# Splitting a table's product between VectorE and GpSimd, loading two factors a table sooner, and moving filling products into the prologue

## The chip, the cores and the metric

The kernel runs on one core of a Trainium2 chip. The metric is the device time of one execution in microseconds; lower is better. TensorE multiplies matrices, VectorE and ScalarE work on tiles, GpSimd does small tiles and indirect transfers, and SyncE's queue (SP) issues most of the loads.

## The reference, cut to what matters

Three stages follow one another: a recurrent attention, a mixture of eight experts, and a dense two-layer network.

```
for t in range(S):                      # S = 768, 4 x 8 heads, 40 x 40 states
    y[t]  = r[t] @ state
    Sa    = state @ a[t]
    state = state * w[t] - outer(Sa, b[t]) + outer(v[t], k[t])
x = attention rows, 3072 x 320
x = gate * eom * (relu(x @ w1[e]) @ w2[e])      # e = argmax(x @ w_gate)
out = g(x @ w_in) @ w_out                       # 320 -> 2048 -> 320
```

The change touches the attention alone.

## The kernel before, in words

The sequence is cut into 12 chunks of 64 steps, and the heads into two halves, so there are 24 steps `s` with 16 heads each (8 in each half of the partitions). What a step needs apart from the state is made ahead of time, in what is called a table here. Table `s` is made by `stepA1(s)` and `stepA1b(s)`, all on VectorE:

- a scan over the factors `w`, backwards, gives `F`, the products of the factors up to the chunk's end (L608, 128x520);
- the reciprocal of eight of its columns goes into `d1` (L612), and the same columns are kept as `e64` (L613);
- a second scan, over the factors and `d1`, gives `e` (L616);
- `kf` is `k` and `b`, each multiplied by `F` (L621, 128x1024, of the form 8 x 2 x 64);
- `g` is `a` multiplied by `e` (L627, 128x512).

TensorE then forms the table's 64x64 products `L` from `kf` and `g` (`a2L`, L637) and transposes `kf` (`a2kbp`, L653). ScalarE copies from them, and VectorE multiplies one of them with a mask (`a2ka`, L646, one input in PSUM). Every fourth table a 32x32 triangular inverse is worked out on VectorE. It is a list of small multiplications (L692) and subtractions (L694) between SBUF tiles. `tick()`, called after most other VectorE instructions, takes one of them from the list, and `due()` runs those that must be done by a given step. The result is transposed (L706) for the products `W` of `slot`.

Eight tables (0 to 7) are made in the prologue. Then `slot(s)` runs for each step. It does the step's own products and those of the step before it, and near its end makes table `s+9`; slot 0 makes table 8 as well. The order on each engine is the order in which the program calls; nothing reorders it. The 17th and later slots make no tables. After the attention come the experts and the dense network, in which TensorE is busy nearly without a break.

The inputs of a table lie in one buffer, `fms[0]`, in three pieces: the factors (columns 0 to 520), `k` and `b` (521 to 1544), and `a` (1545 to 2056). `loadAn()` issues the six transfers of the next table on SP's queue behind the table in work. Each waits there until the instruction that reads the piece is done, and each later one waits behind it. `rzs[1]`, `xt` and others are buffers that the slots use later; ScalarE clears them in the prologue.

`heat(n)` issues `n` products of the identity with itself on TensorE, whose result nobody reads. There are 12 at the start, 8 in slot 0 ahead of the first products `W`, and 4 further on in slot 0.

GpSimd has few instructions in the attention: it clears the lower triangle of the inverse, and from the tenth slot on issues the indirect transfers that scatter rows to the experts.

Of the kernel before, what the change touches and what calls it, by code (L numbers as in the profile page):

```python
# [11 lines left out]
F32 = mybir.dt.float32  # L12
# [8 lines left out]
MUL, ADD, SUB = ALU.mult, ALU.add, ALU.subtract  # L21
P = 128
# [524 lines left out]
def attention(ctx,octx,tc,a,m,ident,rp):  # L547

    nc=tc.nc
    FM,R,VM,VX,VT=a["FM"],a["R"],a["VM"],a["VX"],a["VT"]  # L550
# [6 lines left out]
    ep=early.enter_context(tc.tile_pool(name="early",bufs=1,side="right"))  # L557
# [2 lines left out]
    psL=first.enter_context(tc.tile_pool(name="psL0",bufs=2,space=PSUM))  # L560

    LA=8
    NFM=1; NG=LA+1; NX=2; NR=2
    def persist(n,shape,nm,cp=cp):
        r=[]
        for i in range(n):
            t=cp.tile(shape,F32,name=f"{nm}{i}")
            r.append(t)
        return r
    fms=persist(NFM,[P,521+1024+512],"fm",ep)  # L570
    ones1=ep.tile([P,8,65],F32,name="ones1"); d1=ep.tile([P,8,65],F32,name="d1")
    mask=cp.tile([P,64],F32,name="mask")

    gs=persist(NG-3,[P,8,64],"g")+persist(3,[P,8,64],"gx",ep)
    kas=persist(3,[P,8,64],"kx",ep)+persist(LA-3,[P,8,64],"ka")
    xs=persist(NX,[P,2,4,232],"x")
    rzs=persist(NR,[P,2,4,2,64],"rz")
    mcs=persist(2,[P,8,64],"mc")
    xt=cp.tile([P,4,256],F32,name="xt")
    la=deque(range(NST))  # L580
    def loadAn():
        if la: loadA(la.popleft())
    FMP=(slice(0,521),slice(521,1545),slice(1545,2057))
    def loadA(s):
        c,up=divmod(s,2); f=fms[s%NFM]

        for cs in FMP:
            for sd in range(2): nc.sync.dma_start(out=f[64*sd:64*sd+40,cs],in_=FM[c,up,sd,:,cs])
    for cs in FMP: nc.sync.dma_start(out=fms[0][:,cs],in_=a["F0"][0,:,cs])
    la.popleft()  # L590
    nc.vector.memset(ones1,0.0); nc.vector.memset(ones1[:,:,64:65],1.0)
    nc.gpsimd.memset(d1,0.0)
# [2 lines left out]
    def clear(t):  # L595
        t=t.rearrange("p "+" ".join("abcd"[:len(t.shape)-1])+" -> p ("+" ".join("abcd"[:len(t.shape)-1])+")")
        n=t.shape[1]; m=next(m for m in range(D,0,-1) if n%m==0)
        nc.scalar.copy(t.rearrange("p (a b) -> p a b",b=m),z[:,0:m].unsqueeze(1).to_broadcast([P,n//m,m]))
# [3 lines left out]
    E={};KBt={};NT={};N01={};TT={};E64={};yts={};MT={}  # L602

    KF={}; fence=[None]
    def stepA1(s):
        f=fms[s%NFM]
        F=ep.tile([P,521],F32,tag="F1" if s in (1,3) else "F",name="F",bufs=1)
        nc.vector.tensor_tensor_scan(F[:,519::-1],f[:,520:0:-1],ones1.rearrange("p q t -> p (q t)")[:,::-1],0.0,MUL,ADD)  # L608
        F3=F[:,0:520].rearrange("p (q t) -> p q t",q=8)
        tick()  # L610
        e64=ring.tile([P,8,1],F32,tag="e64",name="e64",bufs=LA+3)
        nc.vector.reciprocal(d1[:,:,0:1],F3[:,:,0:1])  # L612
        nc.vector.tensor_copy(e64,F3[:,:,0:1])  # L613
        tick()
        e=ring.tile([P,8,65],F32,tag="e",name="e",bufs=LA+2)
        nc.vector.tensor_tensor_scan(e.rearrange("p q t -> p (q t)"),f[:,0:520],d1.rearrange("p q t -> p (q t)"),0.0,MUL,ADD)  # L616

        tick()
        if s in (1,3,5): kf=xt.rearrange("p a (b h t) -> p (a b) h t",b=2,h=2)
        else: kf=ep.tile([P,8,2,64],F32,tag="kf",name="kf",bufs=1)  # L620
        nc.vector.tensor_tensor(kf,f[:,521:1545].rearrange("p (q h t) -> p q h t",q=8,h=2),F3[:,:,1:65].unsqueeze(2).to_broadcast([P,8,2,64]),MUL)  # L621
        KF[s]=kf;E[s]=e;E64[s]=e64
        tick()
    def stepA1b(s):
        f=fms[s%NFM]; g=gs[s%NG]; e=E[s]
        A3=f[:,1545:2057].rearrange("p (q t) -> p q t",q=8)
        nc.vector.tensor_tensor(g,A3,e[:,:,0:64],MUL)  # L627
        tick()
    LP={}
    def a2L(s):  # L630
        g=gs[s%NG]; kf=KF[s]
        L=LP[s]=[psL.tile([P,8,64],F32,tag=f"L{i}",name=f"L{i}") for i in range(2)]
        for q in range(8):
            for i in range(2):
                for sd in range(2):
                    h=sd^i; sl=slice(64*sd,64*sd+64)
                    nc.tensor.matmul(L[i][64*h:64*h+64,q],kf[sl,q,h],g[sl,q],start=(q==0),stop=True,skip_group_check=True)  # L637
        if s%4==0: NT[s//4]=ep.tile([P,4,8,32],F32,tag="nt",name="nt",bufs=1)
        N01[s]=ring.tile([P,8,32],F32,tag="n01",name="n01",bufs=LA+1)
    def a2ev(s,sd):  # L640
        L=LP[s][0]; nt=NT[s//4][:,s%4]; n01=N01[s]; b0=64*sd
        nc.scalar.mul(nt[b0:b0+32],L[b0:b0+32,:,0:32],-1.0)
        nc.scalar.mul(nt[b0+32:b0+64],L[b0+32:b0+64,:,32:64],-1.0)
        nc.scalar.copy(n01[b0:b0+32],L[b0:b0+32,:,32:64])
    def a2ka(s):
        nc.vector.tensor_tensor(kas[s%LA],LP[s][1],mask.unsqueeze(1).to_broadcast([P,8,64]),MUL)  # L646
        tick()
    def a2kbp(s):
        kf=KF[s]; r=[]
        for h in range(2):  # L650
            kbp=ps.tile([P,4,128],F32,tag="ps",name="kbp"); r.append(kbp)
            for q in range(4):
                nc.tensor.transpose(kbp[:,q],kf[:,4*h+q].rearrange("p h t -> p (h t)"),ident)  # L653
        return r
    def a2kb(s,r):
        kb=KBt[s]=ring.tile([P,8,128],F32,tag="kb",name="kb",bufs=LA+1)
        for h in range(2): fence[0]=nc.scalar.copy(kb[:,4*h:4*h+4],r[h])
    m.tick=lambda: tick()
    invq=deque(); fine=[]; end=[]; WARM=12
    def tick():  # L660
        if left[0] or rest()<=lim[0]: return
        if not fine and invq: fine.extend(invq.popleft())
        if fine: fine.pop(0)(False)
    def inv(n):
        while fine: fine.pop(0)(False)
        for _ in range(min(n,len(invq))):
            for f in invq.popleft(): f(True)
        if not invq and end: end.pop()()
    lim=[0]
    def rest(): return len(fine)+2*len(invq)  # L670
# [60 lines left out]
    def loadX(s):  # L731
        c,up=divmod(s,2)
        for sd in range(2):
            vl=slice(64-64*sd,128-64*sd)
            nc.sync.dma_start(out=xs[s%NX][vl,sd].rearrange("p a d -> p (a d)"),in_=VX[c,up,sd])

    def loadVT(s):
        c,up=divmod(s,2)
        for j in range(2):
            nc.sync.dma_start(out=xt[64*j:64*j+40,:,64:192],in_=VT[c,up,j].rearrange("d (a t) -> d a t",a=4))  # L740
    def loadR(s):
        c,up=divmod(s,2)
        rz=rzs[s%NR]
        for j in range(2):
            nc.sync.dma_start(out=rz[64*j:64*j+40,j].rearrange("p a b c -> p (a b c)"),in_=R[c,up,j])
# [15 lines left out]
    def slot(s):  # L761
        B=s<NST; Y=s>0; n2=s+LA if s+LA<NST else None
        if B:
            c,up=divmod(s,2)
# [4 lines left out]
            for q in range(8):  # L769
                for sd in range(2):  # L770
                    sl=slice(64*sd,64*sd+64)
                    i=nc.tensor.matmul(R1[sl,q],g[sl,q],mc[sl,q,0:40],start=False,stop=False,skip_group_check=True)
# [14 lines left out]
        if s==0:  # L787
            a2L(LA-1)
            a2ev(LA-1,0)
            stepA1(LA); stepA1b(LA); loadAn(); a2ka(LA-1)  # L790
            heat(8)
        if Y:
            s1=s-1
            c1,up1=divmod(s1,2)
# [88 lines left out]
        if s+LA+1<NST: stepA1(s+LA+1); stepA1b(s+LA+1)  # L883
# [35 lines left out]
    def heat(n):  # L919
        warm=ps.tile([P,512],F32,tag="ps",name="warm")  # L920
        for _ in range(n): nc.tensor.matmul(warm[:,0:128],ident,ident,start=True,stop=True)
    heat(WARM)
    stepA1(0); stepA1b(0); loadAn()
    kbp={}
    for s in range(4):
# [13 lines left out]
    for s in range(4,LA):  # L939
        if s<LA-1:  # L940
            a2L(s)
            for sd in range(2): a2ev(s,sd)
        if s<LA-1: a2kb(s,a2kbp(s))
        if s<LA-1: stepA1(s+1); stepA1b(s+1); loadAn(); a2ka(s)
        inv(4)
    clear(xt); loadVT(0); loadX(1); loadR(1)
    clears=m.clear(z)
    inv(100)
# [5 lines left out]
    for s in range(NST+1):  # L954
        slot(s)
        if s==NST-5: early.close(); m.open(octx)
        if s>NST-5: m.early()
        if s==NST-1: m.first()
# [4 lines left out]
def body(tc,a):  # L963
    nc=tc.nc
    with ExitStack() as ctx, tc.manual_schedule():
        cp=ctx.enter_context(tc.tile_pool(name="cp",bufs=1))
        ident=cp.tile([P,P],F32,name="ident")
        m=Moe(ctx,tc,a,ident,cp)
        rp=ctx.enter_context(tc.tile_pool(name="rp",bufs=1))
        with ExitStack() as actx: rq=attention(actx,ctx,tc,a,m,ident,rp)  # L970
        m.open2(ctx)
        m.go(rq)
# [25 lines left out]
```

## Time and profile before

| | us |
|---|---|
| median of three runs (983.27 to 986.19) | 984.25 |
| the profiled execution | 983.8 |
| its span, first to last instruction | 982.1 |
| TensorE busy | 929.9 |
| VectorE busy | 758.5 |
| GpSimd busy | 154.7 |

Busy times are sums over the whole span. What an engine does in one stage has to be read from the rows of that stage. An engine's instructions start a little before the one in front has ended, so the time that an instruction adds is read from start to start.

### The profile page before, as it was taken

How to read it: one execution, taken by the hardware profiler on the slowest of the kernel's cores; microseconds unless marked ns; L12 is line 12 of the kernel's file. 1: busy time of each engine (PE TensorE's matmuls, PEld its weight loads, DVE VectorE, ACT ScalarE, POOL GpSimd, SP SyncE). 2: the span in 40 equal slices, each digit the busy share in tenths (PEclk: the TensorE clock that was granted, in tenths of full speed). 3: DMA queues.
4: the chain of work that ended last, by engine and by line, in shares of the span. 5: the costliest groups of instructions: out<-in, count | busy, mean ns of one | idle time of the engine just before them, and what ended most of it. 6: DMA issues, size and time to landing. Idle time of an engine off the chain costs nothing. (4 is left out here: it accounts for less than half of the span.)

```text
span 982.1 us, 26651 instructions
## 1 busy us (share of the span) xinstructions
PE 929.9 (95%) x11140; PEld 849.1 (86%) x11140; DVE 758.5 (77%) x1715; ACT 400.1 (41%) x823; POOL 154.7 (16%) x246
## 2 busy tenths in 40 slices
PE   6469999999999999999999999899999999999998
PEld 5458888888889999899999998779999999999997
DVE  7999899999998556688888886677766666666655
ACT  3736445555553443655556554332212221212211
POOL 1000000111011114144434443101010010100000
PEclk7569899999999999999999999899999999999999
DMA  4434677445433643677777766311000010000000
GB/s 125 123 107 152 214 215 233 129 134 144 123 95 95 189 134 108 224 235 231 233 239 230 247 224 193 123 47 28 28 22 33 1 30 25 27 27 1 28 1 27
DMA packets 59390, 118.45 MB, mean 121 GB/s; under 512 B 7492, under 2 KB 34308, under 8 KB 59268
## 3 DMA queue, kind: packets, MB, share of 16 engines
q1 hardware_dynamic: 55220, 103.04, 34.7%
q0 software_dynamic: 4048, 13.69, 4.1%
q8 instruction: 88, 1.44, 0.6%
q14 instruction: 34, 0.28, 0.1%
HBM read 90.24 MB, written 26.46 MB: 119 GB/s over the span
## 5 line engine op out<-in xcount | busy, mean ns | idle before, releaser
L394 PE MATMUL hp<-xh,w 128*128 128x512 f32 (+3 forms) x1008 | 298.9, 379 | 0.5 <-DVEq L248 0.3
L421 PE MATMUL yp<-w,hh 128*128 128x320 f32 (+1 forms) x1280 | 284.3, 309 | 0.6 <-ACT hh L410 0.6
L421 PEld LDWEIGHTS yp<-w,hh 128*128 128x128 f32 (+1 forms) x1280 | 217.0, 185 | 11.5 <-ACT hh L410 2.2
L394 PEld LDWEIGHTS hp<-xh,w 128*128 128x128 f32 x1008 | 188.1, 189 | 27.3 <-DVEq L248 0.5
L421 PE MATMUL yp<-w,hl 128*128 128x320 f32 x584 | 181.5, 311 | 4.6 <-DVE hl L402 4.0
L410 ACT CAST hh<-g 128x512 fp32r<-128x512 f32 x96 | 59.5, 620 | 276.1 <-PE yp L421 148.3
L394 PE MATMUL hp<-xl,w 128*128 128x512 f32 (+3 forms) x336 | 127.2, 379 | 0.2 <-DVE xl L386 0.2
L411 DVE TENSOR_TENSOR hl<-g,hh 128x512 fp32r<-128x512 f32 x96 | 66.5, 692 | 73.4 <-ACT hh L410 73.4
L421 PEld LDWEIGHTS yp<-w,hl 128*128 128x128 f32 x584 | 109.8, 188 | 6.8 <-DVE hl L402 4.9
L408 DVE TENSOR_SCALAR g<-hp,al 128x512 f32<-128x512 f32 x96 | 71.9, 749 | 39.8 <-PE hp L394 39.7
L310 DVE TENSOR_TENSOR w<-raw,w 128x1024 fp32r<-128x1024 f32 (+3 forms) x65 | 87.2, 1343 | 17.7 <-ACT w L309 15.6
L409 DVE SCALAR_TENSOR_TENSOR g<-hp,g 128x512 f32<-128x512 f32 x96 | 66.4, 692 | 3.3
L394 PEld LDWEIGHTS hp<-xl,w 128*128 128x128 f32 x336 | 63.6, 189 | 5.7 <-DVE xl L386 0.6
L309 ACT CAST w<-raw 128x1024 fp32r<-128x1024 f32 (+1 forms) x66 | 64.2, 975 | 8.1 <-DMA raw<-W 8.0
L692 DVE TENSOR_TENSOR tmp<-S 128x30 f32<-128x30 f32 (+27 forms) x258 | 63.9, 273 | 1.0
L694 DVE TENSOR_TENSOR S<-S,tmp 128x30 f32<-128x30 f32 (+27 forms) x258 | 63.8, 272 | 0.9
L508 POOL DMA_INDIRECT xg<-xs,pos x24 | 25.5, 1064 | 228.7 <-PE tp L383 168.4
L814 PE MATMUL Pp<-rz,xt 128*128 128x128 f32 x384 | 55.3, 287 | 0.0
L784 ACT COPY x<-W 32x320 f32<-32x320 f32 x96 | 40.0, 417 | 35.2 <-PE W L781 32.5
L399 ACT ACTIVATE hh<-hp 128x448 fp32r<-128x448 f32 (+2 forms) x72 | 36.6, 508 | 37.5 <-issue 23.4
L815 DVE TENSOR_TENSOR x<-Pp,mask 128x512 f32<-128x512 f32 x48 | 32.6, 687 | 21.2 <-PE Pp L814 16.7
L814 PEld LDWEIGHTS Pp<-rz,xt 128*128 128x128 f32 x384 | 46.4, 191 | 2.5 <-issue 0.2
(169 smaller groups left out, 1359.1 us busy)
## 6 DMA issues: line engine op xcount, KB each, us to landing
raw<-W SPq DMA_DIRECT2D x45, 512.0 KB
x<-VX SPq DMA_DIRECT2D x48, 232.0 KB
fm<-FM SPq DMA_DIRECT2D x46, 160.0 KB
xs<-z SPq DMA_DIRECT2D x5, 1440.0 KB
raw<-WI SPq DMA_DIRECT2D x10, 512.0 KB
raw<-WO SPq DMA_DIRECT2D x10, 512.0 KB
vv<-VM SPq DMA_DIRECT2D x24, 160.0 KB
rz<-R SPq DMA_DIRECT2D x48, 80.0 KB
```

The costliest lines, as they stand in the source:

```text
L309: s.nc.scalar.copy(hi,r[0][:,0:n])
L310: (eng or s.nc.vector).tensor_tensor(lo,r[0][:,0:n],hi.bitcast(F32),SUB)
L394: for i,(l,r) in enumerate(seq): nc.tensor.matmul(hp,l,r,start=(i==0),stop=(i==len(seq)-1))
L408: nc.vector.tensor_scalar(g,hp,0.0,s.al[:,f:f+1],ALU.min,MUL)
L409: nc.vector.scalar_tensor_tensor(g,hp,0.0,g,ALU.max,ADD)
L410: nc.scalar.copy(hh,g)
L411: nc.vector.tensor_tensor(hl,g,hh.bitcast(F32),SUB)
L421: nc.tensor.matmul(yp[j][o],l,r[:,f],start=(f==0 and i==0),stop=(f==nf-1 and i==len(p)-1))
L692: V.tensor_tensor(t3[0][:,r],S[:,r,j:j+1].to_broadcast([P,n,w]),S[:,j:j+1,j+1:].to_broadcast([P,n,w]),MUL)
L694: for r in parts(split): V.tensor_tensor(S[:,r,j+1:],S[:,r,j+1:],t3[0][:,r],ADD)
L784: k=nc.scalar.copy(x[bl,sd,:,64:192].rearrange("p a (j d) -> p a j d",j=2)[:,:,:,0:40],W[bl].rearrange("p (a j) d -> p a j d",j=2))
L814: nc.tensor.matmul(Pp[:,2*qq:2*qq+2],xt[:,qq,128*sd:128*sd+128],rz1[:,:,qq,sd],start=True,stop=True)
```

## The change

Three things are changed. First, `kf` is made by two instructions of half the size, one for `[:,:,1]` on GpSimd, one for `[:,:,0]` on VectorE. GpSimd's half is tied by a wait to the copy of `e64`, which now stands directly in front of the second scan; VectorE's half stays behind the second scan. Second, the factors of tables 1 and 3 go to `rzs[1]` instead of `fms[0]`, and up to table 4 the factors are issued one call of `loadAn()` earlier. Table 1's are issued at the very start, with their padding. Third, 22 filling products are put at the end of the prologue, and those ahead of the first `W` in slot 0 are 4 instead of 8.

```
+    def fw(s): return rzs[1].rearrange(...)[:,0:521] if s in (1,3) else fms[0][:,FMP[0]]
+    def loadP(s,t,cs):
+        c,up=divmod(s,2)
+        for sd in range(2): nc.sync.dma_start(out=t[64*sd:64*sd+40],in_=FM[c,up,sd,:,cs])
     def loadA(s):
-        c,up=divmod(s,2); f=fms[s%NFM]
-        for cs in FMP:
-            for sd in range(2): nc.sync.dma_start(out=f[64*sd:64*sd+40,cs],in_=FM[c,up,sd,:,cs])
+        if s<4 or s>4: loadP(s+1 if s<4 else s,fw(s+1 if s<4 else s),FMP[0])
+        for cs in FMP[1:]: loadP(s,fms[0][:,cs],cs)
     for cs in FMP: nc.sync.dma_start(out=fms[0][:,cs],in_=a["F0"][0,:,cs])
+    nc.sync.dma_start(out=fw(1),in_=a["F0"][1,:,FMP[0]])
...
     def stepA1(s):
-        f=fms[s%NFM]
+        f=fms[0]; w=fw(s)
...
-        nc.vector.tensor_tensor_scan(F[:,519::-1],f[:,520:0:-1],ones1...,0.0,MUL,ADD)
+        nc.vector.tensor_tensor_scan(F[:,519::-1],w[:,520:0:-1],ones1...,0.0,MUL,ADD)
         tick()
         nc.vector.reciprocal(d1[:,:,0:1],F3[:,:,0:1])
-        nc.vector.tensor_copy(e64,F3[:,:,0:1])
         tick()
+        i=nc.vector.tensor_copy(e64,F3[:,:,0:1])
+        j=nc.gpsimd.tensor_tensor(kf[:,:,1],kb[:,:,1],F3[:,:,1:65],MUL)
+        tc.add_manual_dep(j.ins,i.ins.name,...,reason="beside the next scan")
-        nc.vector.tensor_tensor_scan(e...,f[:,0:520],d1...,0.0,MUL,ADD)
+        nc.vector.tensor_tensor_scan(e...,w[:,0:520],d1...,0.0,MUL,ADD)
         tick()
-        nc.vector.tensor_tensor(kf,f[:,521:1545]...,F3[:,:,1:65]...to_broadcast([P,8,2,64]),MUL)
+        nc.vector.tensor_tensor(kf[:,:,0],kb[:,:,0],F3[:,:,1:65],MUL)
...
             stepA1(LA); stepA1b(LA); loadAn(); a2ka(LA-1)
-            heat(8)
+            heat(4)
...
+    heat(22)
     clear(xt); loadVT(0); loadX(1); loadR(1)
```

## Rows read from the trace of the kernel before

**Rows 1.** Windows: stretch, length, busy PE, PEld, DVE, ACT, POOL, granted clock, DMA.

```profile
0.00:73.00 73.00, 41.83 (x718) 37.76 (x719) 66.64 (x160) 34.64 (x72) 5.46 (x37) 0.65 0.41 118
75.00:300.00 225.00, 216.49 (x5205) 194.64 (x5199) 215.19 (x647) 119.50 (x304) 18.57 (x60) 0.98 0.54 160
300.00:350.00 50.00, 50.00 (x1168) 45.90 (x1170) 33.91 (x134) 19.91 (x50) 7.28 (x12) 1.00 0.46 139
```

**Rows 2.** Timeline of VectorE, tables 1, 3, 4: start, length, instruction, idle before.

```profile
9.92 1.24 DVE L608 TENSOR_TENSOR_SCAN F<-fm,ones 128x520 f32<-128x520 f32 x1 [0.96 <-DMA fm<-FM]
...
11.43 1.24 DVE L616 TENSOR_TENSOR_SCAN e<-fm,d 128x520 f32<-128x520 f32 x1
12.59 1.20 DVE L621 TENSOR_TENSOR xt<-fm,F 128x1024 f32<-128x1024 f32 x1
13.71 0.68 DVE L627 TENSOR_TENSOR g<-fm,e 128x512 f32<-128x512 f32 x1
14.31 0.68 DVE L646 TENSOR_TENSOR kx<-L,mask 128x512 f32<-128x512 f32 x1
...
23.26 1.20 DVE L621 TENSOR_TENSOR xt<-fm,F 128x1024 f32<-128x1024 f32 x1
...
27.51 1.24 DVE L616 TENSOR_TENSOR_SCAN e<-fm,d 128x520 f32<-128x520 f32 x1
28.87 1.23 DVE L621 TENSOR_TENSOR kf<-fm,F 128x1024 f32<-128x1024 f32 x1
```

**Rows 3.** Timeline of VectorE and GpSimd among the experts.

```profile
439.91 1.28 POOL L330 TENSOR_TENSOR lf<-lf,qt 128x512 f32<-128x512 f32 x1 [1.71 <-ACT hh L399]
...
440.28 1.99 DVE L310 TENSOR_TENSOR w<-raw,w 128x1024 fp32r<-128x1024 f32 x1
441.28 2.15 POOL L331 TENSOR_TENSOR lf<-lf,qt 128x512 f32<-128x512 f32 x1
```

**Rows 4.** Timeline of VectorE and GpSimd in two slots.

```profile
204.19 1.01 POOL L177 DMA_INDIRECT xs<-xu,pos  x1 [0.45 <-ACT kb L657]
...
218.01 1.24 DVE L608 TENSOR_TENSOR_SCAN F<-fm,ones 128x520 f32<-128x520 f32 x1
218.04 1.99 POOL L177 DMA_INDIRECT xs<-xu,pos  x1 [0.49 <-issue]
219.16 0.33 DVE L694 TENSOR_TENSOR S<-S,tmp 128x184 f32<-128x184 f32 x1
```

**Rows 5.** Timeline of GpSimd and VectorE around 306 us.

```profile
306.00 2.49 POOL L198 COPY gap<-x 1x1 f32<-1x1 f32 x1 [9.95 <-ACT x L784]
306.04 0.47 DVE L692 TENSOR_TENSOR tmp<-S 128x120 f32<-128x120 f32 x2
...
308.36 0.55 DVE L757 TENSOR_TENSOR tm<-MY,mc 128x160 f32<-128x160 f32 x2
```

**Rows 6.** Waits of VectorE, 75 to 300 us: total, times, longest.

```profile
DVE x L815 <- PE Pp L814: 6.7, 9, 1.3
```

**Rows 7.** Timeline of VectorE and TensorE, end of the prologue and slot 0.

```profile
66.11 1.98 DVE L706 STREAM_TRANSPOSE tt<-S 128x1024 f32<-128x1024 f32 x1
...
73.95 2.14 DVE L698 STREAM_TRANSPOSE S<-nt 128x512 f32<-128x512 f32 x2 [0.94 <-ACT nt L643]
...
60.83 1.93 PE L730 MATMUL R<-vv,kx 64*64 64x40 f32 x32 [7.07 <-issue]
...
68.94 2.72 PE L921 MATMUL warm<-ident 128*128 128x128 f32 x16
71.59 0.76 PE L781 MATMUL W<-rh,tt 32*32 32x40 f32 x32
```

**Rows 8.** Timeline of VectorE and TensorE near 99 us; last, the window behind it.

```profile
98.91 1.28 DVE L815 TENSOR_TENSOR x<-Pp,mask 128x512 f32<-128x512 f32 x2
...
99.65 0.39 PE L861 MATMUL MY<-x,kb 128*64 128x104 f32 x2 [1.12 <-DVE x L815]
...
101.10:107.90 6.80, 6.80 (x120) 6.14 (x118) 6.77 (x26) 1.17 (x2) 0.00 (x0) 0.50 0.70 208
```

More of the change, by code (lines that the diff above doesn't have):

```diff
@@ L562, in attention @@
     LA=8
-    NFM=1; NG=LA+1; NX=2; NR=2
+    NG=LA+1; NX=2; NR=2
     def persist(n,shape,nm,cp=cp):
@@ L569, in persist @@
         return r
-    fms=persist(NFM,[P,521+1024+512],"fm",ep)
+    fms=persist(1,[P,521+1024+512],"fm",ep)
     ones1=ep.tile([P,8,65],F32,name="ones1"); d1=ep.tile([P,8,65],F32,name="d1")
@@ L583, in attention, with fw @@
     FMP=(slice(0,521),slice(521,1545),slice(1545,2057))
+    def fw(s): return rzs[1].rearrange("p a b c d -> p (a b c d)")[:,0:521] if s in (1,3) else fms[0][:,FMP[0]]
+    def loadP(s,t,cs):
+        c,up=divmod(s,2)
+        for sd in range(2): nc.sync.dma_start(out=t[64*sd:64*sd+40],in_=FM[c,up,sd,:,cs])
     def loadA(s):
-        c,up=divmod(s,2); f=fms[s%NFM]
-        for cs in FMP:
-            for sd in range(2): nc.sync.dma_start(out=f[64*sd:64*sd+40,cs],in_=FM[c,up,sd,:,cs])
+        if s<4 or s>4: loadP(s+1 if s<4 else s,fw(s+1 if s<4 else s),FMP[0])
+        for cs in FMP[1:]: loadP(s,fms[0][:,cs],cs)
     for cs in FMP: nc.sync.dma_start(out=fms[0][:,cs],in_=a["F0"][0,:,cs])
+    nc.sync.dma_start(out=fw(1),in_=a["F0"][1,:,FMP[0]])
     la.popleft()
@@ L605, in stepA1 @@
     def stepA1(s):
-        f=fms[s%NFM]
+        f=fms[0]; w=fw(s)
         F=ep.tile([P,521],F32,tag="F1" if s in (1,3) else "F",name="F",bufs=1)
-        nc.vector.tensor_tensor_scan(F[:,519::-1],f[:,520:0:-1],ones1.rearrange("p q t -> p (q t)")[:,::-1],0.0,MUL,ADD)
+        nc.vector.tensor_tensor_scan(F[:,519::-1],w[:,520:0:-1],ones1.rearrange("p q t -> p (q t)")[:,::-1],0.0,MUL,ADD)
         F3=F[:,0:520].rearrange("p (q t) -> p q t",q=8)
+        if s in (1,3,5): kf=xt.rearrange("p a (b h t) -> p (a b) h t",b=2,h=2)
+        else: kf=ep.tile([P,8,2,64],F32,tag="kf",name="kf",bufs=1)
+        kb=f[:,521:1545].rearrange("p (q h t) -> p q h t",q=8,h=2)
         tick()
@@ L612, in stepA1 @@
         nc.vector.reciprocal(d1[:,:,0:1],F3[:,:,0:1])
-        nc.vector.tensor_copy(e64,F3[:,:,0:1])
         tick()
+        i=nc.vector.tensor_copy(e64,F3[:,:,0:1])
+        j=nc.gpsimd.tensor_tensor(kf[:,:,1],kb[:,:,1],F3[:,:,1:65],MUL)
+        tc.add_manual_dep(j.ins,i.ins.name,mybir.DependencyInfo(mybir.DependencyClass.Sync,mybir.DependencyReason.DATA),reason="beside the next scan")
         e=ring.tile([P,8,65],F32,tag="e",name="e",bufs=LA+2)
-        nc.vector.tensor_tensor_scan(e.rearrange("p q t -> p (q t)"),f[:,0:520],d1.rearrange("p q t -> p (q t)"),0.0,MUL,ADD)
+        nc.vector.tensor_tensor_scan(e.rearrange("p q t -> p (q t)"),w[:,0:520],d1.rearrange("p q t -> p (q t)"),0.0,MUL,ADD)
         tick()
-        if s in (1,3,5): kf=xt.rearrange("p a (b h t) -> p (a b) h t",b=2,h=2)
-        else: kf=ep.tile([P,8,2,64],F32,tag="kf",name="kf",bufs=1)
-        nc.vector.tensor_tensor(kf,f[:,521:1545].rearrange("p (q h t) -> p q h t",q=8,h=2),F3[:,:,1:65].unsqueeze(2).to_broadcast([P,8,2,64]),MUL)
+        nc.vector.tensor_tensor(kf[:,:,0],kb[:,:,0],F3[:,:,1:65],MUL)
         KF[s]=kf;E[s]=e;E64[s]=e64
@@ L624, in stepA1b @@
     def stepA1b(s):
-        f=fms[s%NFM]; g=gs[s%NG]; e=E[s]
+        f=fms[0]; g=gs[s%NG]; e=E[s]
         A3=f[:,1545:2057].rearrange("p (q t) -> p q t",q=8)
```

## The prediction

> **What bounds the kernel now.** I read the table of windows first, because the shares of the whole span mix stages. In the prologue, the first 73 us, VectorE is busy 66.6 us while TensorE does 41.8 and GpSimd 5.5 [rows 1]: VectorE sets the end there. In the slots from 75 to 300 us VectorE is busy for 215.2 of 225 us and TensorE for 216.5, so both are nearly full, and neither can be shortened by much alone. From 300 us on tables are no longer made and TensorE has no idle time. What TensorE is late by at 300 us therefore stays to the end.
>
> The timeline of VectorE then gives one table. From the second scan's start to `kf` are 1.16 us, from `kf` to `g` 1.12 us, from `g` to the next instruction 0.60 us [rows 2]. The table of waits says that VectorE's idle time in the slots is mostly one wait, 6.7 us on TensorE's `Pp` [rows 6].
>
> The last views to read are timelines of VectorE and GpSimd together, since the change rests on the two working side by side. Where both multiply SBUF tiles, they don't. GpSimd's product of 128x512 takes 1.28 us and ends at 441.19. VectorE's product of 128x1024 begins at 440.28 and takes 1.99 us, though one of this size takes 1.20 us alone [rows 2, 3]. It does its work after 441.19. GpSimd's next product begins at 441.28 and takes 2.15 us; it ends at 443.43, 1.16 us after VectorE's has ended (442.27). So one stands still for as long as the other runs.
>
> **GpSimd's half of `kf`.** VectorE's half is 128x512. I cost it as `g`, of the same size, 0.60 us, against 1.12 us for the whole: 0.52 us saved in each of 24 tables.
>
> GpSimd's half is 128x512 with two SBUF inputs, the form of rows 3. It waits for the copy of `e64`, which takes about a tenth of a us, and the second scan follows that copy on VectorE without a wait. The scan will be running when GpSimd's half begins. No row has a GpSimd product beside a scan. The nearest is a scatter's read: 1.01 us beside a reduction, 1.99 us when a scan has begun 0.03 us ahead of it [rows 4]. It lost 0.98 us, about the length of the scan, and had its turn when the scan was over, although a subtraction of two SBUF tiles followed. Scans, too, shut GpSimd out.
>
> What follows depends on where GpSimd gets in.
> - Early, right behind the scan, as in rows 4: VectorE's half, or the small product that `tick` puts there, stands for 1.16 us. Net: +1.16 - 0.52 = +0.64 us a table.
> - Late: a tiny copy on GpSimd took 2.49 us, from 306.00 to 308.50, until VectorE's run of SBUF products ended and one with an input in PSUM began at 308.36 [rows 5]. In a table that place is the product with the mask (0.60 us, one input in PSUM). Net: -0.52 + 1.16 - 0.60 = +0.04 us. Where the two products with `Pp`, each with an input in PSUM, follow it directly (1.28 us for the pair at 98.91, [rows 8]), all is covered: -0.52 us.
> - Beside the scan after all: -0.52 us.
>
> The Trainium skill speaks against this edit: the page "GPSIMD Engine Reference", section "Specifications", says that GpSimd shares its SBUF interfaces with VectorE and contends with instructions that have two SBUF inputs, which the scan, the half product and `g` all have. By that rule the sum is the serialised one below; without it, it would be the first rival's. Rows 3 agree with it for products, and rows 4 for a scan.
>
> I take the mean of early and late for the four tables 5 to 8, where small products fill the gaps: 0.34 x 4 = +1.4 us. For tables 9 to 23 late lies between +0.04 and -0.52, say -0.24, and the mean with early is +0.2: 15 x 0.2 = +3.0 us. A third of that goes into VectorE's waits for `Pp` [rows 6]: +2.0 us.
>
> **Tables 1 to 4 and the reload.** Here `k` and `b` have a single buffer, and the next table's can't be loaded before `kf` has read them. Table 3's product ends at 24.46. Table 4's begins at 28.87, 1.36 us after its scan's start instead of 1.16, so it waited for the load: about 4.4 us from freed to landed [rows 2]. The loop is 4.4 + 1.2 = 5.6 us. With the change both halves must have read: 4.4 + 0.60 + 1.16 = 6.2 us when GpSimd follows VectorE's half, and 0.6 more if `g` goes first. Four reloads: 4 x 0.55 = 2.2, less 0.5 because the last half is shorter, +1.7 us; or 4 x 1.15 - 0.5 = +4.1 us. I take +2.5, nearer the first by rows 4. The early factors remove the wait of 0.96 us in front of table 1's scan [rows 2], but what VectorE reaches sooner there it spends waiting for `k` and `b`. I count nothing for it, and up to -1.0 if the reload isn't the limit.
>
> Behind the reload on SP's queue stand the table's `a`, needed one product later, and in the slots the next slot's loads, which have several us to spare. Behind GpSimd's waiting half stand its clears and scatters, for which nobody waits within a slot. Moving the `e64` copy past a `tick` costs nothing. The fourth load at the start lies under the first scans.
>
> **Filling products.** Eight products show as 16 passes of 0.17 us, 2.72 us. They hold back `W`, which begins at 71.59 though its `tt` is ready at 66.11 + 1.98 = 68.09 [rows 7]. The new 22 take 44 x 0.17 = 7.5 us, and TensorE sits idle for 7.07 us there, so they cost it at most 0.4. With 4 fewer products ahead of `W` (1.4 us), and a higher clock behind the 22, `W` could begin up to 3.5 us sooner. But `tt` comes from VectorE, which is now 2.5 + 3 x 0.34 = 3.5 us late, so `W` stays where it is. What is left: VectorE's wait of 0.94 us for `nt` [rows 7] is covered, -0.9. If VectorE isn't late, TensorE's start of the slots moves with it.
>
> **The sum.** +2.5 + 1.4 + 2.0 - 0.9 = +5.0 us, on the profiled execution's own 983.8 us (span 982.1 and 1.7 around it; the median of the runs is 984.25): 988.8, forecast 989.
>
> **The rivals.**
> - The scan leaves GpSimd enough room and the half is free. For: a scan takes 1.16 us for 520 columns, about twice a product's time a column, so a fine-grained sharing could let both run. Against: rows 4. Tables 1 to 4: -1.0 - 0.5, since the reload loop, 4.4 + 1.28, stays about as long. Tables 5 to 8: -2.1. The wait for `nt`: -0.9. Slots: 15 x -0.52 = -7.8, but TensorE has only 8.5 us idle of 225, so I count half, -4. Together -8.5: 975 (972 to 980).
> - GpSimd gets in early every time: +1.7 + 4 x 0.64 - 0.9 + 15 x 0.64 - 2 = +11 us: 995. It has a point beyond which it gets worse. TensorE waits 1.12 us at 98.5 for VectorE's `x`, and from 101.1 its clock is granted at 0.5, the lower of its two levels (1.2 GHz of 2.4), for 6.8 us [rows 8]. Another such spell would cost up to 3.4 us: 998.
> - GpSimd gets in late every time: +4.1 + 0.2 - 0.9, and half of 15 x -0.24: +1.6: 985. For it are rows 5, against it rows 4.
>
> **How the numbers follow.** Chances: the mixed, serialised forecast 0.40 (985 to 992), free 0.30, early every time 0.15, late every time 0.15. About 0.3% (981.3 to 987.2) is what a measurement can tell from no change. Faster is 0.27 from free and 0.05 from late: 0.32. Same is 0.03 from free, 0.08 from late, 0.04 from the forecast: 0.15. Slower is the rest, 0.53. The range runs from 974, which leaves out the lower third of free (0.10), to 998 (0.06 above it).
>
> **What would show it.** If I am right, GpSimd's L-line of `kf` takes 2.2 to 4 us instead of 1.28, and VectorE's half, a small product or the next scan near it takes over 1 us longer than alone; tables 2 to 4 begin 5.9 us or more apart; slot 0's `W` begins near 71.6. If the scan and GpSimd's half both keep their lengths (1.24 and 1.28), the step on the scan is wrong and the time is near 975. If GpSimd waits and VectorE's instructions keep their lengths, it got in late. If TensorE's clock falls oftener than at 101 us, the time is at the upper end.

## The result, and the profile after

The changed kernel takes 988.9 us in the median of 15 runs (984.2 to 990.85), against 983.27 us for the kernel before in 15 runs of its own. The ratio is 1.0056, with a 95% interval from 1.0041 to 1.0070: about 5.5 us slower. The execution that was profiled took 990.14 us, with a span of 988.4.

The first line is from the page of the changed kernel; under it are its windows, with the columns of [rows 1].

```profile
PE 935.0 (95%) x11176; PEld 853.6 (86%) x11176; DVE 768.5 (78%) x1715; ACT 399.6 (40%) x823; POOL 202.6 (21%) x270
```

```profile
0.00:73.00 73.00, 44.48 (x754) 40.45 (x755) 66.93 (x157) 34.60 (x72) 21.44 (x45) 0.72 0.40 117
75.00:300.00 225.00, 211.88 (x5026) 190.35 (x5026) 217.01 (x611) 116.46 (x297) 46.91 (x72) 0.97 0.54 157
300.00:350.00 50.00, 50.00 (x1165) 46.02 (x1161) 38.13 (x171) 18.87 (x50) 8.58 (x15) 1.00 0.47 133
```

VectorE was to do 24 x 0.52 us less, and is busy 10.0 us longer (768.5 against 758.5). GpSimd is busy 47.9 us longer, 2.0 us for each of its 24 half products. From 75 to 300 us TensorE does less in the same time than before, 211.9 us against 216.5 [rows 1]: it is the engine that waits.

The timeline of the changed kernel shows where VectorE's time went, in tables 0, 2 and 5, and at the start of table 3's products. The last line is table 5's small product in the kernel before.

```profile
6.00 1.24 DVE L624 TENSOR_TENSOR_SCAN e<-fm,d 128x520 f32<-128x520 f32 x1
6.09 2.13 POOL L621 TENSOR_TENSOR kf<-fm,F 128x512 f32<-128x512 f32 x1 [0.98 <-DVE e L620]
7.16 1.61 DVE L627 TENSOR_TENSOR kf<-fm,F 128x512 f32<-128x512 f32 x1
...
18.41 0.69 DVE L627 TENSOR_TENSOR kf<-fm,F 128x512 f32<-128x512 f32 x1
18.45 1.69 POOL L621 TENSOR_TENSOR kf<-fm,F 128x512 f32<-128x512 f32 x1 [3.89 <-DVE e L624]
19.02 1.67 DVE L633 TENSOR_TENSOR g<-fm,e 128x512 f32<-128x512 f32 x1
...
24.16 0.69 DVE L627 TENSOR_TENSOR xt<-fm,F 128x512 f32<-128x512 f32 x1 [0.20 <-DMA fm<-FM]
...
38.88 1.23 DVE L624 TENSOR_TENSOR_SCAN e<-fm,d 128x520 f32<-128x520 f32 x1
39.10 1.98 POOL L621 TENSOR_TENSOR xt<-fm,F 128x512 f32<-128x512 f32 x1 [3.24 <-DVE e L620]
40.03 1.23 DVE L698 TENSOR_TENSOR tmp<-S 128x150 f32<-128x150 f32 x1
```

```profile
38.39 0.29 DVE L692 TENSOR_TENSOR tmp<-S 128x150 f32<-128x150 f32 x1
```

Read the lengths, not the starts. The scan keeps its 1.24 us. GpSimd's half starts 0.09 us after it and takes 2.13 us, against 1.28 us for a product of this form in [rows 3]: it waits for the scan. In 19 of the 24 tables the half starts while a scan runs, 0.09 to 0.61 us into it, and in all of them it ends 0.96 to 0.98 us after the scan's end: how far the scan had come made no difference. In table 0 VectorE's half comes next and takes 1.61 us instead of 0.69. In table 5 a small inverse product comes next and takes 1.23 us, where it took 0.29 in the kernel before. In tables 1 to 4 both halves start together, behind the scan, in tables 1, 3 and 4 when the load of `k` and `b` lands. VectorE's goes first, and in table 2 `g` takes 1.67 us instead of 0.68. In all 24 tables one instruction of VectorE is longer by 0.9 to 1.0 us.

The waits of the changed kernel from 75 to 300 us, and TensorE's timeline at the end of the prologue, answer to [rows 6] and [rows 7].

```profile
DVE x L821 <- PE Pp L820: 6.0, 6, 2.3
...
PE MY L867 <- DVE x L821: 4.3, 7, 1.5
```

```profile
56.36 5.61 PE L927 MATMUL warm<-ident 128*128 128x128 f32 x44
...
70.55 1.16 PE L927 MATMUL warm<-ident 128*128 128x128 f32 x8
71.64 0.76 PE L787 MATMUL W<-rh,tt 32*32 32x40 f32 x32
```

```profile
69.27 2.03 DVE L712 STREAM_TRANSPOSE tt<-S 128x1024 f32<-128x1024 f32 x1
```

TensorE's wait for VectorE's `x` grew from 1.8 us in the kernel before to 4.3. A wait of 2.2 us for which the profile shows nothing is new as well; the last section comes back to it. The filling products sit where TensorE was idle, and `W` begins at 71.64 instead of 71.59: what they gave is used up by `tt`, which VectorE makes 3.2 us later (its transpose, the line above, starts at 69.27 instead of 66.11).

### The profile page after: what moved, and what is told of

It is laid out like the page before. It is cut to its first block, busy times and chain, and to the rows that moved or that the text cites. A ratio compares the mean times of both kernels' runs of the same rounds, so it can differ in the third digit from the quotient of the medians.

```text
span 988.4 us, 26803 instructions
## 1 busy us (share of the span) xinstructions
PE 935.0 (95%) x11176; PEld 853.6 (86%) x11176; DVE 768.5 (78%) x1715; ACT 399.6 (40%) x823; POOL 202.6 (21%) x270
## 5 line engine op out<-in xcount | busy, mean ns | idle before, releaser
L700 DVE TENSOR_TENSOR S<-S,tmp 128x30 f32<-128x30 f32 (+27 forms) x258 | 69.1, 293 | 0.9
L698 DVE TENSOR_TENSOR tmp<-S 128x30 f32<-128x30 f32 (+27 forms) x258 | 68.4, 290 | 1.0
L621 POOL TENSOR_TENSOR kf<-fm,F 128x512 f32<-128x512 f32 x21 | 40.2, 1917 | 118.6 <-DVE e L620 67.8
```

The costliest lines, as they stand in the source:

```text
L621: j=nc.gpsimd.tensor_tensor(kf[:,:,1],kb[:,:,1],F3[:,:,1:65],MUL)
L698: V.tensor_tensor(t3[0][:,r],S[:,r,j:j+1].to_broadcast([P,n,w]),S[:,j:j+1,j+1:].to_broadcast([P,n,w]),MUL)
L700: for r in parts(split): V.tensor_tensor(S[:,r,j+1:],S[:,r,j+1:],t3[0][:,r],ADD)
```

## The experiments

**Theory.** A GpSimd product and a VectorE instruction with two inputs in SBUF, scans among them, take turns, each for a whole instruction (1.24 us of scan, then 0.98 us of GpSimd's half, then VectorE's product, in the rows above). GpSimd's half waits for the second scan, runs right behind it, and holds up VectorE's next SBUF product for longer than VectorE has saved. **Rivals.** The loss comes from the other two parts of the change; or from the reload of `k` and `b` in the prologue; or GpSimd's product slows VectorE wherever it runs.

**The parts one by one.** The whole of `kf` on VectorE again, the rest of the change kept:

```
-        j=nc.gpsimd.tensor_tensor(kf[:,:,1],kb[:,:,1],F3[:,:,1:65],MUL)
-        tc.add_manual_dep(j.ins,i.ins.name,...)
-        nc.vector.tensor_tensor(kf[:,:,0],kb[:,:,0],F3[:,:,1:65],MUL)
+        nc.vector.tensor_tensor(kf,f[:,521:1545]...,F3[:,:,1:65].unsqueeze(2).to_broadcast([P,8,2,64]),MUL)
```

> The changed kernel with the whole of kf on VectorE again (128x1024, 1.20 us); early factors and filling products stay. Theory (GpSimd's half takes the shared access behind the scan and holds VectorE's next SBUF product by 0.93 us, against 0.52 saved): no VectorE product behind a second scan is longer than alone, and the time falls by some 6 to 8 us from the changed kernel's 989, to 981 to 983, at or a little under the kernel before. Rival 1 (the early factors or the filling products cost the time): it stays within 2 us of 989.

Measured: 0.9988 of the kernel before (0.9964 to 1.0011), 984.7 us beside 984.6. All 24 products of `kf` take 1.20 to 1.23 us (number, and shortest, median and longest in ns, of the two tiles that hold `kf`):

```profile
L625 DVE TENSOR_TENSOR kf<-fm,F x21: 1197/1215/1226, 7.4 to 276.2; 128x1024 f32<-128x1024 f32 x21
L625 DVE TENSOR_TENSOR xt<-fm,F x3: 1216/1224/1226, 13.2 to 38.7; 128x1024 f32<-128x1024 f32 x3
```

Taking GpSimd's half away gives back 1.0056 - 0.9988 = 0.0068 of 983 us, 6.7 us (4 to 9.4 by the two intervals together). The fall is as large as expected; the time itself ended 2 us above the bound of 983, but the kernel before took 1.3 us longer on this chip as well.

The kernel before with GpSimd's half alone (the lines above the other way round, with the copy of `e64` in front of the second scan):

> The kernel before with GpSimd's half of kf alone; loads and filling products as before. Theory: 988 to 992, as slow as the changed kernel or up to 3 us slower, since what the other two parts give is missing; each VectorE product behind the second scan takes 0.9 us longer than alone. Rival 1: within 2 us of 983, because GpSimd's half is not what costs.

Measured: 1.0051 (1.0029 to 1.0073), 990.0 us beside 984.6. This part alone makes the loss.

The kernel before with the filling products alone:

```
-            heat(8)
+            heat(4)
...
+    heat(22)
     clear(xt); loadVT(0); loadX(1); loadR(1)
```

> The kernel before with the filling products moved alone (22 in the prologue, 4 instead of 8 in slot 0). Theory: 981.5 to 983.5; the products W of slot 0 begin about 3 us sooner, near 68.5 us, since VectorE's tt is ready at 68.1, but VectorE fills the slots behind, so that little of it reaches the end. Rival 1: 985 or more, if the filling products cost.

Measured: 0.9993 (0.9972 to 1.0014), 984.3 us beside 984.6. `W` begins at 68.01, 3.6 us sooner, as expected, and nothing of it can be measured at the end. The time lies 0.8 us above the expected range, but not above the kernel before.

```profile
65.72 1.16 PE L921 MATMUL warm<-ident 128*128 128x128 f32 x8
68.01 0.76 PE L781 MATMUL W<-rh,tt 32*32 32x40 f32 x32 [1.13 <-DVE tt L706]
```

The kernel before with the early factors alone (the functions `fw`, `loadP` and `loadA` of the change):

> The kernel before with the factors loaded early alone. Theory: 982 to 983.5; the wait of 0.96 us in front of table 1's scan is gone, and up to 1 us of it is spent again in waiting for k and b. Rival 1: 985 or more, if the early loads delay k and b.

Measured: 0.9981 (0.9962 to 1.0000), 1.9 us faster with an interval that just reaches no change. The transpose that follows table 4 starts at 30.60 instead of 31.22; in front of table 1's product 0.69 us is spent in waiting for `k` and `b`. Neither of these two parts costs anything that can be measured (their intervals end at 1.0014 and 1.0000), so the first rival falls.

**Prologue and slots apart.** The changed kernel with GpSimd's half for tables 0 to 7 alone, and for tables 8 to 23 alone:

```
+        if s<8:          # the other kernel: if s>=8
             j=nc.gpsimd.tensor_tensor(kf[:,:,1],kb[:,:,1],F3[:,:,1:65],MUL)
             tc.add_manual_dep(j.ins,i.ins.name,...)
...
+        if s<8: nc.vector.tensor_tensor(kf[:,:,0],kb[:,:,0],F3[:,:,1:65],MUL)
+        else: nc.vector.tensor_tensor(kf,...)
```

> The changed kernel with GpSimd's half for tables 0 to 7 alone; tables 8 to 23 have the whole product on VectorE. The prediction's sum puts 2.5 + 1.0 us of its 5 on these: 986 to 988. If the reload of k and b is the main loss, nearly all of the 5 us is here: 988 to 990. If the slots are, 984 to 985.5.

> The changed kernel with GpSimd's half for tables 8 to 23 alone; tables 0 to 7 have the whole product on VectorE. The prediction's sum puts 2 to 2.5 us on these: 986 to 988. If the reload in the prologue is the main loss: 984 to 985.5. If all of 16 x 0.4 us comes through: 989 to 991.

Measured: 1.0028 (1.0009 to 1.0048) and 1.0015 (0.9994 to 1.0036). Against 0.9988 without GpSimd's half that is 0.0040 and 0.0027, 3.9 us in the prologue and 2.7 us in the slots, together 6.6 of the 6.7 us. Each of the two is uncertain by 3 us, so by the times alone the slots' share isn't clear of noise (985.7 us lies between two of the expected ranges). The traces make it clear. From the start of the eighth slot (its first products with `mc`) to that of the seventeenth the clock is granted in full in each of these kernels:

| kernels | nine slots, us |
|---|---|
| half behind the scan in these slots: the changed kernel, GpSimd's half alone, tables 8 to 23 alone | 123.7, 123.9, 123.8 |
| whole `kf` on VectorE: the kernel before, whole `kf` in the changed kernel, filling alone, early factors alone, half in tables 0 to 7 alone | 121.9, 122.1, 122.1, 122.1, 121.0 |

Both share the loss, so the reload isn't all of it.

**A longer product.** The changed kernel with the whole of `kf` on GpSimd, and no product of it on VectorE:

```
-        j=nc.gpsimd.tensor_tensor(kf[:,:,1],kb[:,:,1],F3[:,:,1:65],MUL)
+        j=nc.gpsimd.tensor_tensor(kf,kb,F3[:,:,1:65].unsqueeze(2).to_broadcast([P,8,2,64]),MUL)
...
-        nc.vector.tensor_tensor(kf[:,:,0],kb[:,:,0],F3[:,:,1:65],MUL)
```

> The changed kernel with the whole of kf on GpSimd (128x1024), tied to the copy of e64, and no product of it on VectorE. Theory: a product of that size holds the shared access about twice as long, some 2.0 us behind the scan against 1.12 saved, +0.9 us a table: 995 to 1003, and the SBUF product behind the scan (g or a small one) takes about 2 us longer than alone. Rival (the loss is a fixed price of starting GpSimd, or of the wait, not of its length): 981 to 986, since VectorE then saves 1.12 instead of 0.52.

Measured: 1.0168 (1.0144 to 1.0192). The timeline of this kernel in table 5:

```profile
40.66 1.24 DVE L624 TENSOR_TENSOR_SCAN e<-fm,d 128x520 f32<-128x520 f32 x1
40.88 2.97 POOL L621 TENSOR_TENSOR xt<-fm,F 128x1024 f32<-128x1024 f32 x1 [3.49 <-DVE e L620]
41.81 2.22 DVE L697 TENSOR_TENSOR tmp<-S 128x150 f32<-128x150 f32 x1
```

The small product that takes 0.29 us alone takes 2.22 us here and 1.23 us behind the half: 1.93 and 0.94 us lost. Twice the product holds VectorE up twice as long, although VectorE itself has 0.6 us less to do a table. A fixed price of starting GpSimd is excluded.

**Another place.** The early factors, and for tables 8 to 23 GpSimd's half tied to `g`, so that it runs beside VectorE's product with the mask and the two with `Pp`, each with one input in PSUM:

```
+            nc.vector.tensor_tensor(kf[:,:,0],kb[:,:,0],F3[:,:,1:65],MUL)     # s>=8
...
-        nc.vector.tensor_tensor(g,A3,e[:,:,0:64],MUL)
+        i=nc.vector.tensor_tensor(g,A3,e[:,:,0:64],MUL)
+        j=nc.gpsimd.tensor_tensor(kf[:,:,1],kb[:,:,1],F3[:,:,1:65],MUL)       # s>=8
+        tc.add_manual_dep(j.ins,i.ins.name,...)
```

> The kernel before with the factors loaded early, and for tables 8 to 23 alone GpSimd's half of kf, tied to g instead of the copy of e64, so that it runs beside the products with the mask and with Pp, each with one input in PSUM. Theory (only VectorE instructions with two SBUF inputs and GpSimd's product shut each other out): GpSimd's product starts behind g, those products beside it keep 0.69 us, at most 0.4 us of a small product behind them is lost, VectorE is done sooner by 0.1 to 0.5 us a table, and the time is 978.5 to 982, at or under that of the early factors alone (982). Rival (GpSimd's product slows VectorE wherever it runs): those products take 0.9 us longer, and the time is 985 to 989.

Measured: 0.9953 (0.9935 to 0.9971), 978.2 us beside 982.4. Its timeline in tables 9 and 11 and its window from 75 to 300 us:

```profile
81.31 1.18 POOL L636 TENSOR_TENSOR kf<-fm,F 128x512 f32<-128x512 f32 x1 [5.11 <-DVE g L634]
81.32 0.68 DVE L656 TENSOR_TENSOR kx<-L,mask 128x512 f32<-128x512 f32 x1
81.92 0.74 DVE L704 TENSOR_TENSOR S<-S,tmp 128x150 f32<-128x150 f32 x1
...
108.45 0.69 DVE L656 TENSOR_TENSOR kx<-L,mask 128x512 f32<-128x512 f32 x1
108.77 1.18 POOL L636 TENSOR_TENSOR kf<-fm,F 128x512 f32<-128x512 f32 x1 [10.59 <-PE R L844]
109.05 1.32 DVE L825 TENSOR_TENSOR x<-Pp,mask 128x512 f32<-128x512 f32 x2
```

```profile
75.00:300.00 225.00, 218.06 (x5317) 196.69 (x5315) 213.20 (x670) 121.50 (x309) 37.04 (x76) 1.00 0.55 162
```

The same product now takes 1.18 us, and VectorE's with an input in PSUM keep their 0.69. Only where a small SBUF product follows does it lose 0.44 us (0.74 instead of 0.30). TensorE gets through 218.1 us of work in the 225, against 216.5 in the kernel before and 211.9 in the changed one. In all 16 tables GpSimd's half takes 1.17 to 1.22 us and the product with the mask at most 0.69. GpSimd's product doesn't slow VectorE wherever it runs, so the last rival falls too.

The kernel before with nothing but this:

> The kernel before with nothing but GpSimd's half of kf for tables 8 to 23, tied to g, so that it runs beside products with an input in PSUM. Theory: the same GpSimd product that costs 2.7 us in the slots behind the scan now gives 1 to 4 us: 979 to 982 against 983 of the kernel before. Rival (GpSimd's half costs wherever it runs, and the gain of the run before came from the early factors): 984 to 987.

Measured: 0.9970 (0.9952 to 0.9989), 2.9 us faster, from the product that costs 2.7 us behind the scan. The mean clock that its runs were granted is that of the kernel before, 0.971 against 0.970 (and 0.969 against 0.970 in the runs of GpSimd's half alone), so a different mean clock explains neither this gain nor that loss. Where the gain comes from is shown in part only. The profiled execution is the fastest of the 12, 7.2 us shorter than that of the kernel before. The nine slots of the table take 121.2 us in it, 0.7 less. Nearly all the rest lies in the seven slots before them, in which the kernel before has a stretch at the lower clock [rows 8] and a wait without a known cause (last section), and this execution has neither.

The same with early factors, and the filling products as in the change:

> The early factors, GpSimd's half tied to g for tables 8 to 23, and the filling products moved as in the change. Theory: the filling products gave nothing by themselves, and VectorE now has more room in the slots, so at most 1.5 us more than without them: 977 to 979.5. Rival (VectorE was all that kept TensorE's earlier start from paying): 974 to 976.

Measured: 0.9922 (0.9902 to 0.9942), 977.6 us beside 984.6: the fastest of all against its own runs of the kernel before. Against 0.9953 without the filling products it is 3 us more, twice what was expected, but the two intervals still overlap. Its runs also had more clock, 0.981 in the mean against 0.971.

And the early factors with the late half, without the small product behind the product with the mask:

```
         nc.vector.tensor_tensor(kas[s%LA],LP[s][1],mask...,MUL)
-        tick()
+        if s<LA-1: tick()
```

> The early factors and GpSimd's half tied to g for tables 8 to 23, without the small product that may follow the product with the mask from table 7 on (it is done later). Theory: a small product there loses 0.45 us behind GpSimd; without it the products with Pp come next, nothing is lost in most slots, and the time is 0.5 to 2 us under that of the same kernel with it: 976.5 to 978.5. Rival (TensorE sets the slots by now): the same within 0.5 us.

Measured: 0.9954 (0.9941 to 0.9968), the same as with it. The 0.44 us are gone from the trace. VectorE's wait for `Pp` takes their place, 13.4 us from 75 to 300 us (first line, this kernel) against 9.0 (second line, with the small product): VectorE now waits for TensorE there, as the rival had it, and the theory's 0.5 to 2 us were wrong.

```profile
DVE x L825 <- PE Pp L824: 13.4, 13, 2.7
```

```profile
DVE x L825 <- PE Pp L824: 9.0, 9, 2.3
```

## Why the prediction was right, step by step

- **The scan shuts GpSimd out: right, on thin evidence.** It rested on one scatter's read of [rows 4]. The scatter of 1.01 us that is set against it as "beside a reduction" had a scan beside it too, for 0.67 us of its length, and was no longer for it:

```profile
204.53 1.23 DVE L608 TENSOR_TENSOR_SCAN F<-fm,ones 128x520 f32<-128x520 f32 x1
```

That scan began 0.34 us behind the scatter, the other 0.03 us ahead of it, so the reading holds for a scan that is already running, which is the case of the half. In the changed kernel every half that starts beside a scan takes 1.6 to 2.1 us. The runs with GpSimd's half behind the scan and behind `g` show it as the cause. The rule of the Trainium skill ("GPSIMD Engine Reference", section "Specifications") named VectorE instructions with two SBUF inputs; the trace agrees, 1.61 us against 0.69 for such a product, and 0.69 for one with an input in PSUM.
- **Where GpSimd gets in: wrong in half.** The sum took the mean of early and late. It was early in every table, which is the condition of the rival at 995 us (chance 0.15). [Rows 5], a tiny copy shut out for 2.49 us by small products, did not repeat: no half waited for the product with the mask.
- **What early costs: too high by 0.24 us.** The sum had 1.16 us of standing, from a GpSimd product that started behind another; measured are 0.92 (1.61 - 0.69). The half ends 0.98 us behind the scan, while the same product takes 1.18 us beside PSUM products, so some 0.2 us of its start lies under the scan. So early is +0.40 us net a table, not +0.64. The signs set for it were too large for the same reason: 2.2 to 4 us for the half (measured 1.6 to 2.1) and over 1 us for VectorE's product (0.9 to 1.0).
- **That 988.8 is so near is luck in part.** The two errors, too little early and too dear, nearly cancel for tables 5 to 8 (0.34 taken, 0.40 measured). For tables 9 to 23 they don't (0.20 against 0.40); there less of the time came through to the end than the two thirds that the sum let through.
- **Tables 1 to 4: right in kind.** The inverse's transpose behind table 4 begins at 32.98 (first line, the changed kernel) instead of 31.22 (second line, before): +1.8 us, where +2.5 was taken and +1.7 was the lower bound. With GpSimd's half alone it begins at 32.57, +1.4 us.

```profile
32.98 2.08 DVE L704 STREAM_TRANSPOSE S<-nt 128x1024 f32<-128x1024 f32 x1
```

```profile
31.22 2.11 DVE L698 STREAM_TRANSPOSE S<-nt 128x1024 f32<-128x1024 f32 x1
```

GpSimd's half of table 2 ends at 18.45 + 1.69 = 20.14, and the next table's begins at 24.16, with the reload between: 4.0 us rather than 4.4 (3.9 and 4.3 for the tables beside it). The second scans of tables 2, 3 and 4 follow their forerunners by 6.33, 5.59 and 5.74 us; "5.9 us or more" held for the first alone. The whole of the prologue was 2.5 + 1.0 = 3.5 us in the sum and 3.9 us, uncertain by 3, in the runs; VectorE's `tt` is 3.2 us late in the traces.
- **The slots: right in size.** 0.34 + 2.0 = 2.3 us in the sum, 2.7 us in the runs, of 16 x 0.40 = 6.4 us gross. The nine slots from the eighth on, where neither profile has a fall of the clock, take 123.7 us instead of 121.9 before: 0.2 us a slot, half of the 0.40.
- **What is late at 300 us stays to the end: not exactly.** The seventeenth slot begins 8.2 us later than before (292.67 against 284.52), the end comes 6.3 us later (spans of 988.4 and 982.1). From that slot on the profiles of all kernels take 695.7 to 701.1 us, and TensorE does wait among the experts, for VectorE above all. The sum has no term for that.
- **The early factors: counted as nothing.** By themselves they give 0 to 3.7 us. Table 4 is 0.6 us sooner with them alone, but not in the kernel with the whole `kf` on VectorE, which has them too (31.28). Whether they are worth anything isn't settled.
- **The filling products: right for this change.** `W` begins at 71.64; 71.6 was written. VectorE's wait for `nt` (-0.9) is gone, but also in the kernel with GpSimd's half alone, so VectorE's lateness covers it, not the filling. That they become worth something once VectorE has room is likely from the last runs, and not settled.
- **The sign of the clock: it came, without its price.** The clock of the changed kernel's profile falls to the lower level three times in the slots (about 88 to 92, 102 to 105 and 143 to 150 us) instead of once, but the time is not near 998. The profile of GpSimd's half alone has no such fall from 75 to 300 us (1.00) and that kernel is as slow: the loss doesn't need the clock.
- **The free rival** (975 us, chance 0.30) is excluded by the lengths. What it hoped for is there in another place.

## What to carry to other kernels

Before work is given to GpSimd to relieve VectorE, look at what VectorE does beside it: two products on SBUF tiles don't run at once (0.9 us lost for each GpSimd product of 128x512 here), and a scan counts as one of them. Put such work beside VectorE instructions that read PSUM, which kept their 0.69 us here. A reader can tell from the trace alone, by comparing the lengths of the same instruction with and without the other engine at work; busy time hides it, since the standing instruction counts as busy.

## What the runs showed of the hardware that had not been expected

GpSimd's waiting product gets its turn right behind a scan although VectorE's next SBUF product is ready: in each of the 19 tables where the half started beside the scan, VectorE's half takes 1.61 us instead of 0.69, or the small product that comes next takes 0.9 us longer than alone. In [rows 5] a one-element copy got none in 2.49 us of small products. What decides between the two isn't settled here.

In most profiles TensorE has a wait between 115 and 160 us in which the profile shows nothing that it waits for: 0.9 us in the kernel before, 2.2 in the changed one, up to 2.2 in the others (in some there are two such waits), 0.2 in the early factors with GpSimd's half behind `g`, and none in two of the experiments (the kernel before with GpSimd's half behind `g` alone, and that half with the early factors and the filling products). With the 22 filling products the long one stands in the middle of the 32 products `W`, with the old ones in the middle of the 32 products of `x` and `n` that come some 36 passes later in the program. 18 more filling products are 36 passes (22 show as 44), so the wait stands at about the same count of TensorE's passes, whatever they work on. Here it is in the kernel with the whole `kf` on VectorE, with the window behind it.

```profile
135.82 0.74 PE L785 MATMUL W<-rh,tt 32*32 32x40 f32 x16 [2.08 <-issue]
```

```profile
135.40:142.20 6.80, 6.38 (x67) 5.98 (x68) 2.23 (x6) 2.29 (x6) 0.00 (x0) 0.50 0.29 96
```

The clock is granted at 0.50, the lower level, behind it, and that slot takes 19.8 us; in the changed kernel it takes 20.0, in the kernel before 15.8. In the kernel with the filling products alone the wait is 1.89 us, the window behind it (134.6 to 141.4) has a clock of 1.00, and the slot takes 16.7 us. Such a spell is thus worth 3 us, nearly half the spread of a kernel's runs (984.2 to 990.85 for the changed one), and a single profile of two kernels should not be subtracted where it lies in one of them. What makes the wait is open.
